# Attention followed by a soft mixture of experts: a new order of all engines, chosen PSUM banks and copy engines, and more second buffers

## The chip, the cores and the metric

The kernel runs on one core of a Trainium2 chip. The metric is the device time of one execution in microseconds (us), lower is better. One profiled execution gives the trace; the times beside it are from runs of the same program.

## The reference, cut to what matters

```python
def _attn_ref(q, k, v):                    # 8 batches, 8 heads, 576 positions, 64 channels, fp32
    scores = (1.0 / np.sqrt(D)) * np.matmul(q, k.transpose(0, 1, 3, 2))
    mask = block_i >= block_j              # blocks of 64 positions: 9 block rows, block-causal
    scores = np.where(mask, scores, -1000000000.0)
    ...
    attn = np.exp(scores - max); attn = attn / (attn.sum(-1) + 1e-09)
    return np.matmul(attn, v)

def _moe_ref(x, phi, w1, w2):              # x: 4608 tokens x 512; 8 experts, 4 slots each, F = 1024
    logits = x @ phi                       # 4608 x 32
    d = softmax(logits, axis=0)            # over all tokens
    slot_input = d.T @ x                   # 32 x 512
    for e in range(E):
        slot_out[e] = np.maximum(slot_input[e] @ w1[e], 0.0) @ w2[e]
    c = softmax(logits, axis=1)            # over the slots
    return c @ slot_out
```

The tokens of x are the attention output of all batches, with the heads side by side.

## The kernel before, in words

**Two stages.** The first goes through 32 pairs (8 batches of 4 pairs; a pair is two heads of one batch, side by side in the 128 partitions). The second computes the experts and the output.

**A pair.** TensorE makes the scores in three steps: `qk(m, "7")` (called UA below, line 412) for query blocks 6 and 7, `qkb` (UB, line 433) for blocks 8, 3, 2, 1 and 0, `qk(m, "5")` (UC, line 412) for blocks 4 and 5. VectorE (DVE) takes the row maxima (`rowmax`, line 454), ScalarE (ACT) the exponentials with their sums (`expo`, line 464), GpSimd (POOL) scales the probabilities by the inverse sums (`norm`, line 481). TensorE then transposes the probabilities in four groups, g7, g5, gc and gd (`tr`, line 501), into an even and an odd PSUM bank, and ACT or DVE copies each bank to SBUF (`evac`, lines 339 and 341). From the copies TensorE forms the product with V: `pv` in two halves pv0 and pv1 (line 539), and `pv8` (called pa, line 549) for block 8. `evac_x` copies the results to xT (xa, xb).

**A batch.** After its four pairs come the logits (`part`, `part4`: lines 568 and 579), a running softmax over tokens (`stats`, `stats1`, `stats2`), x with the tokens in the partitions (`xnat`, line 682, and its copies `evac_n`), and the sums over tokens (`slots`, `slots4`: lines 702 and 711). These are spread over the pairs of the next batches; only those of the last batch stand alone at the end of the stage.

**The experts.** 32 pieces of weights, 1 MB each, W0 to W31. W0 to W15 are read by `up` (line 947), W16 to W31 by `down` (line 967). RES pieces have a place of their own in the big SBUF tile `arena` and are loaded during the attention. The rest go where attention's buffers were, in the order of their places, when those are free (lines 818 to 826), and from W24 on where a used piece of `up` was. `emit` (lines 924, 909) forms the output and copies it to a used piece, from where it is written.

**The order** of all engines is written out: every step is put in a list with a number from the table TM (line 66; per pair of a batch, with entries of their own for pairs 0 to 3, as A to D, and for the last two, w and y), the list is sorted, and the engines' queues follow it. Each engine runs its queue in order. EN says which engine makes a copy.

**PSUM** has eight banks of 128x512: two for products (`x`), two for scores (`sc`), a double one for the scores of blocks 8 and 5 (`sc8`), two for transposes (`pt_e`, `pt_o`). In pair 0 the transposes' banks also hold the scores of blocks 3 to 0.

**At the start** eight products of zeros (`warm`, line 380) and later 8 and 12 short ones (`fill`, line 387) have no use in the result. The eight stand at fixed numbers from -50 up:

```python
        for i in range(WARM):
            at(-50 + 0.01 * i, warm, i)
```

Of the kernel before, what the change touches and what calls it, by code (L numbers as in the profile page):

```python
# [8 lines left out]
F32 = mybir.dt.float32  # L9
# [11 lines left out]
NP = H // 2  # L21
# [17 lines left out]
ONE = "82"  # L39
NXT = 6  # L40
WARM = 8
RES = 17
# [3 lines left out]
for name, n in (  # L46
    *((f"x{i}", S) for i in XIN), ("kr", S), ("q0", S), ("ks0", S), ("p7_0_0", 512), ("p7_1_0", 512),
    ("p5_0_0", 384), ("p5_1_0", 384),
    ("p3_0", 256), ("p1_0", 128), ("p0_0", 128), ("q1", S), ("ks1", S), ("p8", 640), ("v0", 640),
    ("p3_1", 256), ("p2", 256), ("p1_1", 128), ("p0_1", 128),  # L50
    *((f"p{t}_{j}_1", 64 * t + 64) for t in (7, 5) for j in range(2)),
    ("v1", 640), ("pt0", PTN), ("pt1", PTN), ("phi", 128),
):
    AREAS[name] = (LATE0, LATE0 + n)
    LATE0 += n
# [31 lines left out]
    16.10454, "UCC": 16.10654, "nm71C": 16.30906, "xbA": 34.86058, "paB": 25.66258, "rm3C": 16.65299, "ogdB":  # L87
# [7 lines left out]
    24.75602, "gcC": 24.75802, "egcC": 24.76002, "ogcC": 24.76202, "gdC": 24.76402, "paC": 24.76602, "ex8D":  # L95
# [946 lines left out]
```

## Time and profile before

| | us |
|---|---|
| three runs | 364.75, 365.13, 367.5 |
| median | 365.13 |
| span of the profiled execution | 363.1 |
| median less that span | 2.0 |

The page gives the profiled execution by its span, from its first to its last instruction; it gives no other time for it. The granted TensorE clock was 0.988 of full speed in the mean. In the rows further down, a matmul of fp32 is four instructions in the trace (x4), a transpose one. "idle before" says what ended an engine's idle time.

### The profile page before, as it was taken

How to read it: one execution, taken by the hardware profiler on the slowest of the kernel's cores; microseconds unless marked ns; L12 is line 12 of the kernel's file. 1: busy time of each engine (PE TensorE's matmuls, PEld its weight loads, DVE VectorE, ACT ScalarE, POOL GpSimd, SP SyncE). 2: the span in 40 equal slices, each digit the busy share in tenths (PEclk: the TensorE clock that was granted, in tenths of full speed). 3: DMA queues.
4: the chain of work that ended last, by engine and by line, in shares of the span. 5: the costliest groups of instructions: out<-in, count | busy, mean ns of one | idle time of the engine just before them, and what ended most of it. 6: DMA issues, size and time to landing. Idle time of an engine off the chain costs nothing.

```text
span 363.1 us, 14318 instructions
## 1 busy us (share of the span) xinstructions
PE 347.6 (96%) x5694; PEld 237.8 (65%) x5694; DVE 269.1 (74%) x756; ACT 268.0 (74%) x855; POOL 205.6 (57%) x473
## 2 busy tenths in 40 slices
PE   8899999999999999999999999999999999999983
PEld 3566676767667767776677676767676766437651
DVE  4877767978897888778877887788778866463442
ACT  3877889887988798879888988898888776022342
POOL 4886577757765776676666666666667473000000
PEclk9999999999999999999999999999999999999995
DMA  6766363754473646553845464626413069999887
GB/s 202 215 190 209 101 190 123 226 172 138 148 281 102 180 134 215 140 177 99 296 136 148 142 226 125 206 72 245 133 47 118 12 237 382 380 422 420 353 340 281
DMA packets 29219, 72.29 MB, mean 199 GB/s; under 512 B 6881, under 2 KB 15201, under 8 KB 24161
## 3 DMA queue, kind: packets, MB, share of 16 engines
q1 hardware_dynamic: 29152, 71.38, 57.1%
q8 instruction: 45, 0.74, 0.8%
q14 instruction: 22, 0.17, 0.1%
HBM read 61.93 MB, written 9.44 MB: 197 GB/s over the span
## 4 chain that ended last, share of the span: by engine, by line
PE 62%; DVE 5%; ACT 1%; issue 1%; POOL 0%; DVEq 0%; ACTq 0%
PE x L539 13%; PE sc L412 10%; PE pt_e L501 9%; PE sc L433 5%; PE x L549 4%; PE so L967 4%; PE hp L947 4%; PE o L924 3%; PE pt_o L501 2%; DVE arena L341 2%; PE x L702 2%; PE x L568 2%; DVE stat L454 1%; PE x L682 1%; PE x L579 1%
## 5 line engine op out<-in xcount | busy, mean ns | idle before, releaser
L481 POOL TENSOR_SCALAR arena<-arena,stat 128x512 f32<-128x512 f32 (+6 forms) x288 | 152.2, 544 | 57.2 <-DVE stat L470 39.0
L464 ACT ACTIVATE arena<-sc,stat 128x512 f32<-128x512 f32 (+6 forms) x282 | 150.5, 546 | 9.0 <-DVE stat L454 7.9
L454 DVE TENSOR_REDUCE stat<-sc 128x1 f32<-128x512 f32 (+4 forms) x251 | 129.8, 543 | 8.5 <-PE sc L433 5.6
L501 PEld LDWEIGHTS pt_e<-ident,arena 64*128 64x128 f32 x789 | 60.9, 138 | 35.9 <-POOL arena L481 13.5
L501 PE MATMUL pt_e<-ident,arena 64*128 64x64 f32 x789 | 75.2, 228 | 5.4 <-DVE arena L341 2.3
L539 PE MATMUL x<-arena 128*64 128x128 f32 (+2 forms) x640 | 76.2, 384 | 0.2
L501 PE MATMUL pt_o<-ident,arena 64*128 64x64 f32 x789 | 74.8, 229 | 0.2
L412 PE MATMUL sc<-arena 64*128 64x512 f32 (+1 forms) x252 | 63.0, 581 | 0.2
L501 PEld LDWEIGHTS pt_o<-ident,arena 64*128 64x128 f32 x789 | 59.7, 138 | 3.2 <-ACT arena L339 2.1
L539 PEld LDWEIGHTS x<-arena 128*64 128x64 f32 x640 | 41.1, 136 | 30.2 <-issue 18.2
L464 ACT ACTIVATION_READ_ACCUMULATOR arena<-sc,stat 128x1 f32 x282 | 58.4, 207 | 0.0
L339 ACT COPY arena<-pt_o 128x384 f32<-128x384 f32 (+1 forms) x87 | 44.4, 510 | 16.6 <-PE pt_o L501 14.4
L341 DVE COPY arena<-pt_e 128x384 f32<-128x384 f32 (+2 forms) x72 | 40.9, 567 | 10.3 <-PE x L539 7.4
L433 PE MATMUL sc<-arena 64*64 64x192 f32 (+2 forms) x752 | 43.3, 341 | 0.2 <-ACT arena L464 0.2
L433 PEld LDWEIGHTS sc<-arena 64*64 64x64 f32 x752 | 36.2, 132 | 8.3 <-ACT arena L464 3.2
L339 ACT COPY arena<-pt_e 128x384 f32<-128x384 f32 (+2 forms) x54 | 26.7, 494 | 16.6 <-PE pt_o L501 14.0
L474 POOL TENSOR_SCALAR stat<-stat 128x2 f32<-128x2 f32 (+1 forms) x96 | 18.7, 195 | 31.3 <-ACT arena L464 26.3
L470 DVE RECIPROCAL stat<-stat 128x2 f32<-128x2 f32 (+1 forms) x96 | 15.4, 167 | 24.5 <-POOL stat L474 23.6
L549 PE MATMUL x<-arena 128*64 128x64 f32 x640 | 25.7, 227 | 0.0
L549 PEld LDWEIGHTS x<-arena 128*64 128x64 f32 x640 | 21.3, 137 | 5.6 <-ACT xn L339 3.3
L373 POOL TENSOR_SCALAR arena<-arena 128x576 f32<-128x576 f32 x32 | 21.5, 671 | 5.9 <-DMA arena<-in_k 3.0
L341 DVE COPY arena<-pt_o 128x384 f32<-128x384 f32 (+2 forms) x39 | 20.6, 528 | 3.9 <-PE pt_o L501 1.7
(167 smaller groups left out, 362.5 us busy)
## 6 DMA issues: line engine op xcount, KB each, us to landing
arena<-in_w SPq DMA_DIRECT2D x32, 1024.0 KB, 6.9
arena<-in_k SPq DMA_DIRECT2D x32, 288.0 KB, 3.3
arena<-in_q SPq DMA_DIRECT2D x32, 288.0 KB, 3.1
arena<-in_v SPq DMA_DIRECT2D x32, 256.0 KB, 3.2
out<-arena SPq DMA_DIRECT2D x7, 1024.0 KB, 5.1
arena<-in_v SPq DMA_DIRECT2D x32, 32.0 KB, 3.2
out<-arena SPq DMA_DIRECT2D x2, 512.0 KB, 4.5
out<-arena SPq DMA_DIRECT2D x4, 256.0 KB, 3.8
```

The costliest lines, as they stand in the source:

```text
L339: nc.scalar.copy(out=out, in_=in_)
L341: nc.vector.tensor_copy(out=out, in_=in_)
L373: nc.gpsimd.tensor_scalar(out=area(f"ks{m % NQB}"), in0=area("kr" if m > 1 else f"ks{m}"), scalar1=SCALE, scalar2=0.0, op0=ALU.mult, op1=A ...
L412: nc.tensor.matmul(scores(t + str(j), m), lhsT=q[r, lo:lo + 128], rhs=k[r, 0:NC[t]], start=True, stop=True)
L433: nc.tensor.matmul(o, lhsT=a, rhs=b, start=True, stop=True)
L454: nc.vector.tensor_reduce(out=st[:, 0, u:u + n], in_=sc, axis=AX.XY if x == "8" else AX.X, op=ALU.max, negate=True)
L464: nc.scalar.activation(out=pr, in_=sc, func=AF.Exp, bias=st[:, 0, u:u + 1], accum_out=st[:, 1, u:u + 1],)
L474: nc.gpsimd.tensor_scalar(out=st[:, 2, c], in0=st[:, 1, c], scalar1=EPS, scalar2=1.0, op0=ALU.add, op1=ALU.mult)
L481: nc.gpsimd.tensor_scalar(out=pr, in0=pr, scalar1=st[:, 2, u:u + 1], scalar2=0.0, op0=ALU.mult, op1=ALU.add)
L501: nc.tensor.transpose(out=trbank(m, g)[i][:, 64 * n:64 * n + 64], in_=prob(m, x)[r, 128 * c:128 * c + 128], identity=ident[r, r],)
L539: nc.tensor.matmul(xps[m, 0][64 * j:64 * j + 64, lo:hi], lhsT=vs(m)[:, j, c, :], rhs=rhs, start=a, stop=z, skip_group_check=True,)
L549: nc.tensor.matmul(xps[m, 1][64 * j:64 * j + 64, 0:64], lhsT=vs(m)[:, j, c, :], rhs=arena[:, lo:lo + 64], start=(c == 0), stop=(c == NQ - 1),)
```

## The change

The tables TM and EN are new: all engines have another order, and many copies another engine. A table BK names the PSUM bank of each kind of step for each kind of pair. The scores of blocks 8 and 2 get a second buffer (`p8_0`, `p8_1`, `p2_0`, `p2_1`), and so do the transposed probabilities (`pt0_0` to `pt1_1`). These take 4096 columns of `arena`; RES goes from 17 to 15, and nine pieces instead of seven are loaded into attention's buffers at the end. WARM and `fill`'s counts are as before.

```diff
-ONE = "82"
+ONE = ""
+NPT = 2
 NXT = 6
 WARM = 8
-RES = 17
+RES = 15
...
-    ("p3_0", 256), ("p1_0", 128), ("p0_0", 128), ("q1", S), ("ks1", S), ("p8", 640), ("v0", 640),
-    ("p3_1", 256), ("p2", 256), ("p1_1", 128), ("p0_1", 128),
+    ("p3_0", 256), ("p1_0", 128), ("p0_0", 128), ("q1", S), ("ks1", S), ("p8_0", 640), ("p8_1", 640), ("v0", 640),
+    ("p3_1", 256), ("p2_0", 256), ("p2_1", 256), ("p1_1", 128), ("p0_1", 128),
...
-    ("v1", 640), ("pt0", PTN), ("pt1", PTN), ("phi", 128),
+    ("v1", 640), *((f"pt{j}_{i}", PTN) for i in range(NPT) for j in range(2)), ("phi", 128),
...
-    "T": 9.2, "lkA": -5.94771, "lqA": -2.81305, "lkB": -10.95031, "lqB": -8.91013, "ksA": 2.22677, "UAA":
...
-        xbk = [ps.tile([128, 512], F32, name=f"x{i}") for i in range(2)]
...
-        scm = [ps.tile([128, 512], F32, name=f"sc{j}") for j in range(2)]
-        scn = ps.tile([128, 1024], F32, name="sc8")
...
-        ptb = [ps.tile([128, 512], F32, name=f"pt_{x}") for x in "eo"]
...
+        duo = [
+            ps.tile([128, 1024], F32, name=f"duo{i}") if i in WIDE else [ps.tile([128, 512], F32, name=f"one{i}{j}") for j in range(2)]
+            for i in range(4)
+        ]
...
+        def bank(key, z):
+            return BK.get(key + z, BK.get(key))
...
         def warm(i):
             if i == 0:
-                xps["w"] = xbank("pb")
+                xps["w"] = one(0)
...
         def trbank(m, g):
-            return scm if m == NB * NP - 1 and g in ("gc", "g5") else ptb
+            return two(bank("T" + g, sfx(m)))
...
         def evac(m, g, i):
-            lo = AREAS["pt0"][0]
+            lo = AREAS[f"pt0_{m % NPT}"][0]
...
-                pt = arena[:, AREAS[f"pt{j}"][0]:AREAS[f"pt{j}"][1]]
+                pt = area(f"pt{j}_{m % NPT}")
```

Of the new table, `WIDE = (2,)`; in pairs 4 to 29 (kinds .0 to .3) the scores stand in banks 1 (`one10`, `one11`) and 2 (`duo2`), the transposes in 3 (`one30`, `one31`), the products in `one00` (for pa of one kind in `one01`), which are the places that `sc`, `sc8`, `pt` and `x` were.

**TensorE, from the start.** `idle` are the zeros of `warm` and `fill`; sc and sc8 (now one1 and duo2) hold scores, x0 (now one00) the product's bank. Before:

```order
L380 LDWEIGHTS idle_78
L380 MATMUL x0_106<-idle_78 128x512
...
L412 MATMUL sc0_108<-arena_58 128x512
L412 MATMUL sc1_109<-arena_58 128x512
L433 MATMUL sc8_110<-arena_58 64x288 x2
...
L412 MATMUL x0_106<-arena_58 128x384
L412 MATMUL x1_107<-arena_58 128x384
L387 LDWEIGHTS idle_78
L387 MATMUL x0_106<-idle_78 128x128
```

Now:

```order
L448 MATMUL one10_108<-arena_58 128x512
L448 MATMUL one11_109<-arena_58 128x512
L469 MATMUL duo2_110<-arena_58 64x288 x2
...
L415 LDWEIGHTS idle_78
L415 MATMUL one00_106<-idle_78 128x512
...
L448 MATMUL one00_106<-arena_58 128x384
L448 MATMUL one01_107<-arena_58 128x384
L422 LDWEIGHTS idle_78
L422 MATMUL one00_106<-idle_78 128x128
```

UA and UB of pair 0 stand ahead of the warm-ups now. Six warm-ups follow, then UA of pair 1, UC of pair 0, both runs of `fill`, the last two warm-ups and UB of pair 1.

**VectorE, in pairs 0 and 1.** The first two rows are maxima of pair 0's blocks 5, the rows stat1 those of pair 1's UB; a copy of 2x4x64 empties a bank of pair 0's g7. Before:

```order
L454 TENSOR_REDUCE stat0_113<-x0_106 128x1
L454 TENSOR_REDUCE stat0_113<-x1_107 128x1
L341 COPY arena_58<-pt_e_111 128x2x4x64
L454 TENSOR_REDUCE stat1_114<-sc8_110 128x1
L454 TENSOR_REDUCE stat1_114<-sc0_108 128x1
L454 TENSOR_REDUCE stat1_114<-sc1_109 128x1
L341 COPY arena_58<-pt_e_111 128x320
```

Now:

```order
L491 TENSOR_REDUCE stat0_113<-one00_106 128x1
L491 TENSOR_REDUCE stat0_113<-one01_107 128x1
L491 TENSOR_REDUCE stat1_114<-duo2_110 128x1
L491 TENSOR_REDUCE stat1_114<-one10_108 128x1 x2
L491 TENSOR_REDUCE stat1_114<-one11_109 128x1 x2
L507 RECIPROCAL stat0_113<-stat0_113 128x2
L507 RECIPROCAL stat1_114<-stat1_114 128x2
L376 COPY arena_58<-one30_111 128x2x4x64
L376 COPY arena_58<-one31_112 128x2x4x64
```

Both copies of g7 are VectorE's now (the odd one was ScalarE's), and both stand behind all maxima of pair 1's UB.

**VectorE, after the last batch's logits.** bm are the batch's maxima, xn the tokens' x, fident the merge, dn the dispatch weights. Before:

```order
L596 TENSOR_REDUCE bm_7_5335<-x1_107 128x1
L597 TENSOR_REDUCE bm_7_5335<-x1_107 128x1
L626 STREAM_TRANSPOSE c_all_80<-lt_7_5333 128x128
L627 STREAM_TRANSPOSE c_all_80<-lt_7_5333 64x32
L604 TENSOR_TENSOR mrun1_91<-mrun0_90,bm_7_5335 128x2
L605 TENSOR_TENSOR bm_7_5335<-mrun1_91,mrun0_90 128x2
L341 COPY xn_119<-sc8_110 128x8x64
L651 TENSOR_REDUCE fident_95<-sc0_108 1x32
L654 COPY fident_95<-fident_95 1x96
L341 COPY dn_120<-pt_e_111 128x96
```

Now:

```order
L633 TENSOR_REDUCE bm_7_5337<-one00_106 128x1
L634 TENSOR_REDUCE bm_7_5337<-one00_106 128x1
L763 SCALAR_TENSOR_TENSOR acc4_82<-acc4_82,bm_6_4919,duo2_110 128x128
L641 TENSOR_TENSOR mrun1_91<-mrun0_90,bm_7_5337 128x2
L642 TENSOR_TENSOR bm_7_5337<-mrun1_91,mrun0_90 128x2
L376 COPY xn_119<-one10_108 128x8x64
L376 COPY xn_119<-one30_111 128x4x64
L376 COPY xn_119<-one31_112 128x4x64
L689 TENSOR_REDUCE fident_95<-one10_108 1x32
L692 COPY fident_95<-fident_95 1x96
L376 COPY dn_120<-one00_106 128x96
```

The two transposes of the logits have gone behind the end of this chain; a sum of the batch before and two copies of xn have come into it.

## Rows read from the trace of the kernel before

**Rows 1.** The page, part 1: busy us (share of the span), instructions.

```profile
PE 347.6 (96%) x5694; PEld 237.8 (65%) x5694; DVE 269.1 (74%) x756; ACT 268.0 (74%) x855; POOL 205.6 (57%) x473
```

**Rows 2.** Windows: stretch, its length, busy us by engine, PE clock, DMA share, GB/s.

```profile
147.00:183.75 36.75, 36.25 (x613) 25.94 (x611) 30.36 (x87) 31.19 (x103) 25.01 (x57) 1.00 0.57 184
294.00:311.30 17.30, 16.24 (x264) 11.03 (x260) 11.88 (x34) 9.09 (x27) 7.45 (x17) 1.00 0.94 372
311.30:350.40 39.10, 38.59 (x712) 21.47 (x712) 16.78 (x32) 11.24 (x22) 0.00 (x0) 1.00 0.93 382
350.40:354.00 3.60, 2.36 (x19) 1.37 (x19) 1.41 (x5) 1.37 (x5) 0.00 (x0) 1.00 0.94 383
354.00:363.10 9.10, 3.37 (x24) 1.79 (x24) 2.43 (x6) 1.91 (x5) 0.00 (x0) 0.51 0.71 283
```

**Rows 3.** Timeline, TensorE's start: start, us, engine, line, operation, out<-in, count, idle before.

```profile
0.99 3.60 PE L380 MATMUL x<-idle 128*128 128x512 bf16 x8 [0.99 <-DVE mrun L252]
4.51 1.88 PE L412 MATMUL sc<-arena 64*128 64x512 f32 x4
6.32 0.46 PE L433 MATMUL sc<-arena 64*64 64x288 f32 x2
7.57 0.92 PE L412 MATMUL x<-arena 64*128 64x384 f32 x4
8.42 0.62 PE L387 MATMUL x<-idle 128*128 128x128 bf16 x8
8.97 1.13 PE L412 MATMUL sc<-arena 64*128 64x512 f32 x4
10.03 0.84 PE L387 MATMUL x<-idle 128*128 128x128 bf16 x12
12.62 1.31 PE L433 MATMUL sc<-arena 64*64 64x256 f32 x20 [0.24 <-ACT arena L464]
15.69 0.80 PE L549 MATMUL x<-arena 128*64 128x64 f32 x20
17.69 1.11 PE L412 MATMUL sc<-arena 64*128 64x512 f32 x4
```

**Rows 4.** The chain that ended last, UB in the middle: start, us, what.

```profile
131.71 1.25 PE sc L433 x16
```

**Rows 5.** Timeline, DVE in pairs 0 and 1.

```profile
12.87 0.68 DVE L341 COPY arena<-pt_e 128x512 f32<-128x512 f32 x1
13.54 1.09 DVE L454 TENSOR_REDUCE stat<-sc 128x1 f32<-128x576 f32 x3
15.07 0.41 DVE L454 TENSOR_REDUCE stat<-sc 128x1 f32<-128x256 f32 x1
16.34 0.35 DVE L454 TENSOR_REDUCE stat<-sc 128x1 f32<-128x192 f32 x1
```

**Rows 6.** Timeline, TensorE: gd waiting in pairs 0, 1, 5 and 14.

```profile
15.17 0.24 PE L501 MATMUL pt_e<-ident,arena 64*128 64x64 f32 x1 [0.78 <-DVE stat L470]
24.04 0.27 PE L501 MATMUL pt_e<-ident,arena 64*128 64x64 f32 x1 [0.51 <-ACT arena L339]
60.44 0.24 PE L501 MATMUL pt_e<-ident,arena 64*128 64x64 f32 x1 [0.60 <-ACT arena L339]
143.62 0.24 PE L501 MATMUL pt_e<-ident,arena 64*128 64x64 f32 x1 [0.34 <-DVE arena L341]
```

**Rows 7.** The chain that ended last, after the last batch's logits.

```profile
304.95 0.33 ACT lt L339
305.31 0.29 DVE bm L596
305.73 0.22 DVE c_all L626
305.96 0.22 DVE c_all L627
```

**Rows 8.** Timeline, SP's DMA issues at the end.

```profile
293.48 26.03 SPq L284 DMA_DIRECT2D arena<-in_w  x15
```

More of the change, by code (lines that the diff above doesn't have):

```diff
@@ L290, in tile_attention_softmoe, with one, two, sfx @@
         ps = c1.enter_context(tc.tile_pool(name="ps", bufs=1, space=PSUM))
-        xbk = [ps.tile([128, 512], F32, name=f"x{i}") for i in range(2)]
-        scm = [ps.tile([128, 512], F32, name=f"sc{j}") for j in range(2)]
-        scn = ps.tile([128, 1024], F32, name="sc8")
-        ptb = [ps.tile([128, 512], F32, name=f"pt_{x}") for x in "eo"]
-        def xbank(key, z=""):
-            return xbk[EN["X" + key + z]]
+        duo = [
+            ps.tile([128, 1024], F32, name=f"duo{i}") if i in WIDE else [ps.tile([128, 512], F32, name=f"one{i}{j}") for j in range(2)]
+            for i in range(4)
+        ]
+        def one(i):
+            d, j = duo[i // 2], i % 2
+            return d[:, 512 * j:512 * j + 512] if i // 2 in WIDE else d[j]
+        def two(i):
+            return [one(2 * i), one(2 * i + 1)]
+        def sfx(m):
+            return late(m) or f".{m % NP}"
+        def bank(key, z):
+            return BK.get(key + z, BK.get(key))
+        scm = two(1)
+        for t, i in sorted({(k[1], i) for k, i in BK.items() if k[:2] in ("S5", "S7")}):
+            for x in two(i) if EN["Q" + t] == "q" else ():
+                nc.vector.memset(x[0:64, NC[t] - 64:NC[t]], NEG)
         def endz(b):
-            return "z" * (b == NB - 1)
+            return {NB - 1: "z", NB - 2: "v"}.get(b, "")
         def area(name):
@@ L320, in pads @@
                 return
-            for x, n in (("8", 640), ("2", 256), ("0_0", 128), ("0_1", 128)):
+            for x, n in (("8_0", 640), ("2_0", 256), ("8_1", 640), ("2_1", 256), ("0_0", 128), ("0_1", 128)):
                 nc.gpsimd.memset(area("p" + x)[:, NC[x[0]]:n], 0.0)
@@ L393, in scores @@
         def scores(x, m):
-            if m == 0 and x[0] == "5":
-                return xbk[int(x[1])][:, 0:384]
+            z = sfx(m)
             if x == "8":
-                return scn.rearrange("p (n c) -> p n c", n=2)[:, :, 0:288]
-            if x[0] == "5":
-                j = int(x[1])
-                return scn[:, 512 * j:512 * j + 384]
-            if x[0] == "7":
-                return scm[int(x[1])]
+                return duo[bank("S8", z)].rearrange("p (n c) -> p n c", n=2)[:, :, 0:288]
+            if x[0] in "57":
+                return two(bank("S" + x[0], z))[int(x[1])][:, 0:NC[x[0]]]
             j, lo = {"3": (0, 0), "0": (0, 256), "2": (1, 0), "1": (1, 192)}[x]
-            return (scm if m else ptb)[j][:, lo:lo + NC[x]]
+            return two(bank("SB", z))[j][:, lo:lo + NC[x]]
         def qk(m, t):
             q, k = area(f"q{m % NQB}"), area(f"ks{m % NQB}")
-            for j in range(2):
-                r = slice(64 * j, 64 * j + 64)
-                lo = {"7": 0, "5": 128}[t]
-                nc.tensor.matmul(
-                    scores(t + str(j), m), lhsT=q[r, lo:lo + 128], rhs=k[r, 0:NC[t]], start=True, stop=True
-                )
+            lo, n = {"7": 0, "5": 128}[t], NC[t]
+            if EN["Q" + t] == "h":
+                todo = [(slice(0, 128), 0, n)]
+            else:
+                todo = [(slice(0, 64), 0, n - 64), (slice(64, 128), 0, n)]
+            for o, a, e in todo:
+                for j in range(2):
+                    r = slice(64 * j, 64 * j + 64)
+                    nc.tensor.matmul(
+                        scores(t + str(j), m)[o, a:e], lhsT=q[r, lo + o.start:lo + o.stop], rhs=k[r, a:e], start=True, stop=True
+                    )
         def qkb(m):
@@ L424, in qkb @@
                 for i in range(2):
-                    halves[i].append((scn[r, 512 * i:512 * i + 288], q[r, 512:576], k[r, 288 * i:288 * i + 288]))
+                    halves[i].append((scores("8", m)[r, i, :], q[r, 512:576], k[r, 288 * i:288 * i + 288]))
                     o = slice(64 - 64 * j, 128 - 64 * j)
@@ L440, in rowmax @@
             st, u = stat[m % 2], COL[x if x != "5" else "50"]
-            if x == "5":
-                if m:
-                    todo = [(u, 2, scn.rearrange("p (j c) -> p j c", j=2)[:, :, 0:384])]
-                else:
-                    todo = [(u + j, 1, scores(f"5{j}", m)) for j in range(2)]
-                for _, n, sc in todo:
-                    nc.vector.memset(sc[0:64, :, 320:384] if n == 2 else sc[0:64, 320:384], NEG)
+            if x == "5" and bank("S5", sfx(m)) in WIDE:
+                todo = [(u, 2, duo[bank("S5", sfx(m))].rearrange("p (j c) -> p j c", j=2)[:, :, 0:384])]
+            elif x == "5":
+                todo = [(u + j, 1, scores(f"5{j}", m)) for j in range(2)]
             else:
                 todo = [(u, 1, scores(x, m))]
-                if x[0] == "7" and tm(m, "rm" + x) == min(tm(m, "rm70"), tm(m, "rm71")):
+            if EN.get("Q" + x[0]) == "h":
+                if x == "5":
+                    for _, n, sc in todo:
+                        nc.vector.memset(sc[0:64, :, 320:384] if n == 2 else sc[0:64, 320:384], NEG)
+                elif (tm(m, "rm" + x), x) == min((tm(m, f"rm7{j}"), f"7{j}") for j in range(2)):
                     for j in range(2):
-                        nc.vector.memset(scm[j][0:64, 448:512], NEG)
+                        nc.vector.memset(scores(f"7{j}", m)[0:64, 448:512], NEG)
             for u, n, sc in todo:
@@ L522, in pv @@
         def pv(m, i):
-            first = tm(m, f"pv{i}") < tm(m, f"pv{1 - i}")
+            first = (tm(m, f"pv{i}"), i) < (tm(m, f"pv{1 - i}"), 1 - i)
             if first:
-                xps[m, 0] = xbank("pb")
+                xps[m, 0] = one(bank("PB", sfx(m)))
             for j in range(2):
-                pt = arena[:, AREAS[f"pt{j}"][0]:AREAS[f"pt{j}"][1]]
+                pt = area(f"pt{j}_{m % NPT}")
                 if i == 0:
@@ L544, in pv8 @@
         def pv8(m):
-            xps[m, 1] = xbank("pa", "y" * (m == NB * NP - 1))
+            xps[m, 1] = one(bank("PA", sfx(m)))
             for c in range(NQ):
                 for j in range(2):
-                    lo = AREAS[f"pt{j}"][0] + PT8 + 64 * c
+                    lo = AREAS[f"pt{j}_{m % NPT}"][0] + PT8 + 64 * c
                     nc.tensor.matmul(
@@ L562, in part @@
         def part(b, p):
-            z = "z" * (b == NB - 1)
+            z = endz(b)
             order = sorted(range(NP), key=lambda i: TM[f"prt{i}{z}"])
             if p == order[0]:
-                mo[b, "xlg"] = xbank("lg", endz(b))
+                mo[b, "xlg"] = one(bank("LG", endz(b)))
             for g in range(4):
@@ L631, in natural @@
                 r = slice(64 * i, 64 * i + 64)
-                nc.tensor.transpose(out=ptb[i][:, o:o + 64], in_=dt[r, lo:lo + 128], identity=ident[r, r])
+                nc.tensor.transpose(out=two(bank("ND", endz(b)))[i][:, o:o + 64], in_=dt[r, lo:lo + 128], identity=ident[r, r])
         def dispatch(b):
+            ptb = two(bank("ND", endz(b)))
             copy("dn", dn[:, 0:3, :], ptb[0][:, 0:96].rearrange("p (i s) -> p i s", s=NS), endz(b))
@@ L673, in xnat @@
         def xnat(b, i):
-            bk = xbk if b < NB - 1 else (scm, (scn[:, 0:512], scn[:, 512:1024]), ptb)[i]
+            bk = two(bank(f"N{i}", endz(b)))
             mo[b, "xxn", i] = bk
@@ L696, in slots @@
         def slots(b):
-            p0 = xbank("si", endz(b)) if b != NB - 2 else scn[:, 0:512]
+            p0 = one(bank("SI", endz(b)))
             mo[b, "xsi"] = p0
@@ L707, in slots4 @@
         def slots4(b):
-            p0 = xbank("si4") if b != NB - 2 else ptb[0][:, 256:384]
+            p0 = one(bank("S4", endz(b)))
             mo[b, "xsi4"] = p0
@@ L789, in tile_attention_softmoe @@
             if k[-1] == "z":
-                at(tb + TM[k] + 0.0005, fill, scm[1], n)
+                at(tb + TM[k] + 0.0005, fill, one(FZ), n)
             else:
@@ L793, in tile_attention_softmoe @@
         for (m, k), n in FILL0.items():
-            at(m * T + tm(m, k) + 0.00002, fill, xbk[0][:, 384:512], n)
+            at(m * T + tm(m, k) + 0.00002, fill, one(FB)[:, 384:512], n)
         for i in range(RES):
```

36 lines of the change are left out of this document (20 added, 16 removed), and 242 rows, old and new, of tables (BK, EN, TM).

## The prediction

> **What bounds the kernel now.** I read the page's busy times first. TensorE is busy 96% of the span, DVE and ACT 74% each, POOL 57% [rows 1]: see that one engine is near full and two others have a quarter to spare. A mean hides stages, so I read windows next. One round of four pairs in the middle takes 36.75 us, and TensorE is busy 36.25 us of it at the full clock [rows 2]. So in the middle TensorE can give back at most 0.5 us a round, whatever the other engines do; the order can only remove its idle time, since the products and transposes are the same ones. From 294 to 311.3 us TensorE is busy 16.2 of 17.3 us, and in the experts 38.6 of 39.1 [rows 2]. Only the last 12.7 us are loose (2.4 of 3.6 us, then 3.4 of 9.1 at a granted clock of 0.51) [rows 2], and the change leaves that code as it is. What is left is the start, before TensorE is full, and the hand-over to the experts. I read these in the timelines of TensorE and DVE and in the chain of waits.
>
> **The change, part by part.**
>
> *The warm-ups at the start.* Before, eight products of zeros run while the first q and k are on their way, from 0.99 to 4.51 us, where UA of pair 0 starts [rows 3]. They cost nothing there. UA still takes 1.81 us (4.51 to 6.32), against 1.06 for the next one (8.97 to 10.03) and 1.11 for the third, so it runs at the lower level of 1.2 GHz; UB takes 1.25 us (6.32 to 7.57) [rows 3], as in the middle of the kernel [rows 4], so by then the clock is at 2.4 GHz. Now UA and UB come first. Nothing that they wait for is earlier, so UA starts at 4.51 us again, with no work done before it. UB then costs 1.25 us at the upper level or 2.50 at the lower one; these are the bounds. I take 2.50, since the nearest row, UA, ran at the lower level even after eight products. The Trainium skill, TensorE: Matmul & The Clock Gate, section What's actually happening, says that the default state is the throttled one and that activity releases it; by that rule UB costs the 2.50 as well, and by the lower bound of the rows the start would be 1.25 us cheaper.
>
> The warm-ups now have to run while work waits behind them. The eight took 3.5 us at the lower level, 0.44 each; six cost 2.6 us there or 1.3 at the upper. I take 1.3. Then come UA of pair 1 (1.06), UC of pair 0 (0.85, 7.57 to 8.42), both fills (0.55 and about 0.8 us) [rows 3] and two warm-ups (0.4). UB of pair 1 can start at 4.5 + 1.8 + 2.5 + 1.3 + 1.06 + 0.85 + 1.35 + 0.4 = 13.8 us. Before, it got going at 12.62 us, held by ACT [rows 3]: **1.2 us later** (bounds 0, where ACT holds it anyway, and 2.6).
>
> *Copies behind the maxima.* g7 of pair 0 fills both transpose banks, and gd cannot write there until both are empty. Before, ACT emptied one and DVE the other, at 12.87 us, ahead of the maxima of pair 1's UB [rows 5], and gd got through at 15.17 us [rows 6]. Now both copies are DVE's and stand behind all five maxima. UB of pair 1 ends at 13.8 + 1.25 = 15.05. The maxima take 1.09 for three, 0.41 and 0.35 [rows 5], two small reciprocals some 0.3, the copies 0.68 each [rows 5]: gd is free at 15.05 + 1.85 + 0.3 + 1.36 = 18.6 us. Between gd's going on at 15.17 and UA of pair 2 at 17.69 lie 2.5 us before, with pa (0.80) and UC (0.85) in them [rows 3], so 0.9 for gd and g5. Now UA of pair 2 comes at 18.6 + 0.9 = 19.5, 1.8 us later than 17.69, and with pa (0.8) still to do. **The start is 2.6 us behind** (this contains the 1.2). TensorE is nearly full from there on, so the lag is kept unless a later wait of before goes. Bounds: 0, where these copies find DVE free earlier, and 4, where UB is at the late end of its bounds.
>
> *Pairs 1 to 5.* In pairs 1, 2 and 5 gd follows gc directly into the same banks and waits for gc's copies: 0.51 us in pair 1, 0.60 in pair 5 [rows 6]. The new order puts UC, UB or half of pv between them, or takes other banks. In pairs 1 to 3 the new order also puts copies of gc and g5 behind maxima on DVE, the same pattern as above, so I count gain against loss there: 0 (from -1.0, both waits gone, to +1.0, a wait of the size of one copy and one maximum more). In pair 5: **-0.6 us**.
>
> *The middle.* TensorE's order is nearly the same, with pv's halves or `part`s exchanged, and gc ahead of UB in one pair of four; in every kind of pair the banks are those of before, under new names. ACT and DVE have 24 copies each per round, before and now. The second buffers of p8, p2 and pt remove waits that POOL, ACT and DVE may have, but no wait of TensorE that the windows show. The one clear wait there, 0.34 us before gd in the fourth pair of a round [rows 6], keeps its order and its banks. So 0; bounds -0.34 and +0.34 for each of six rounds, -2.0 and +2.0, since nothing excludes a new wait of that size.
>
> *The last batch.* After the last logits the chain goes through DVE. It waits 0.36 us for ACT's copy of the logits, and two transposes take 0.45 [rows 7]. Both leave the chain now: -0.8. A sum of 0.25 and two copies of 256 columns (about 0.4 each by the copy of 512, 0.68 [rows 5]) come into it: +1.05. I take **+0.2** (bounds -0.8 and +1.05).
>
> *Two more late pieces of weights.* They are 2 x 1.05 MB, at 372 to 382 GB/s about 5.5 us of transfers in a stretch that moves data at a share of 0.94 and 0.93 of all DMA engines [rows 2]. SP issued the 15 pieces from 293.48 us over 26 us [rows 8], as places came free. What is idle there is 6% of 17.3 and 7% of 39.1 us, 3.8 us in all. The new order hands the first four places over early (x, k, q and the first pt buffer), so I let the cover hold: 0. Without it, 5.5 - 3.8 = 1.7 us remain, and these would push the output's writes at the end.
>
> Sum: 2.6 + 0 - 0.6 + 0 + 0.2 + 0 = **+2.2 us** on the profiled execution's span of 363.1 us. The median, 365.13 us, is 2.0 above that span; I add the 2.2 to it: 367.3 us. A change of less than 1% (3.65 us) is about what a measurement of this kernel cannot tell from none.
>
> **The rivals.**
>
> *The splits pay and the copies are in time.* The lag of the start stops at UB's 1.2 us, because DVE finishes its maxima earlier than my row-by-row walk, and TensorE has other transposes to do. Then the waits of pairs 1, 2 and 5 go (-1.6, pair 2 counted like pair 1) and half of the middle's (-1.0): 365.13 - 1.4 = 363.7 us, not slower. It decides where UA of pair 2 starts before about 18.5 us. For it: DVE has a quarter of its time free [rows 1]. Against it: DVE runs in order, and those two copies cannot pass the maxima. If the middle's 0.5 us a round go entirely as well, 361.3.
>
> *The clock.* The start now has TensorE waiting more often: for DVE's copies before gd, for ACT before UC. At the end of the kernel the granted clock fell to 0.51 after a stretch in which TensorE was busy 2.4 of 3.6 us [rows 2]. If the same happens around 16 to 20 us, or if the upper level is not reached until then, some 4 to 5 us of products take twice as long: 367.3 + 4 = 371.3 us. The Trainium skill, TensorE: Matmul & The Clock Gate, section HAM oscillation, warns of just this: gaps between groups of matmuls close the gate, and the next group starts cold. By that rule this rival's time holds; in the trace of before the start has waits too (0.78 us before gd in pair 0 [rows 6]), and its later products show the upper level, which speaks against.
>
> *DMA sets the end.* The last pieces come 1.7 to 5.5 us later and the output's writes behind them; the share of 0.71 after 354 us [rows 2] takes 2.6 us of that up. 367.3 + 1.7 to 2.9, say 369.4 us. Against it: the experts read their pieces in the order of loading, and 15 of 17 places are free when they were before.
>
> **How the numbers follow.** My forecast, the lag kept: 0.50, 367.3 us, its own range 365.8 to 369.0. Splits pay: 0.24, 361.3 to 365.0. Clock: 0.13, 370 to 372. DMA: 0.10, 368.8 to 370.2. Something that no row shows: 0.03. The range that leaves out a tenth on each side is 364.2 to 370.6 us. Slower than 368.8: the clock, most of DMA and a tenth of the forecast, 0.28. Faster than 361.5: a quarter of the splits' case, 0.07. Within 1%: 0.65.
>
> **What would show it.** UB of pair 0 in the new timeline at 2.5 or 1.25 us; UB of pair 1 at 13.8; the wait before gd of pair 0, on DVE's copies; UA of pair 2 at 19.5. A round in the middle at 36.75 us. The last weight piece and the writes behind it no later than before, measured from the start of the experts. I am wrong if the start is not behind by two us when pair 4 begins, or if rounds in the middle change by more than 0.3 us: then some wait that I took for fixed work of TensorE was not.

## The result, and the profile after

The changed kernel takes **368.16 us** (median of 4 runs, 367.55 to 371.41), the kernel before 365.15 beside it: the ratio is 1.0101, with a 95% interval of 1.0069 to 1.0134. The forecast was 367.3, with a range of 364.2 to 370.6. The profiled execution after took 368.23 us, with a span of 366.5 (366.45 in the trace, 363.13 before, so 3.3 longer).

The page of the changed kernel, part 1, answers to [rows 1]:

```profile
PE 345.8 (94%) x5694; PEld 239.3 (65%) x5694; DVE 271.6 (74%) x768; ACT 263.8 (72%) x843; POOL 205.8 (56%) x475
```

TensorE does the same 5694 instructions in 1.8 us less of busy time, while the span grows, so its share falls. The windows after, each over the stage that [rows 2] shows for before (length, busy us of PE, PEld, DVE, ACT, POOL, clock, DMA share, GB/s):

```profile
147.00:183.75 36.75, 36.07 (x611) 26.10 (x611) 30.06 (x87) 30.59 (x100) 24.82 (x57) 1.00 0.50 158
297.10:314.20 17.10, 15.36 (x274) 10.49 (x270) 11.35 (x36) 8.10 (x23) 6.70 (x13) 1.00 0.98 402
314.20:353.30 39.10, 38.51 (x704) 21.43 (x705) 17.59 (x34) 11.20 (x22) 0.29 (x1) 1.00 1.01 414
357.00:366.50 9.50, 2.73 (x32) 1.50 (x28) 2.80 (x6) 2.37 (x6) 0.00 (x0) 0.81 0.74 298
```

The middle and the hand-over have more idle time on TensorE, and in the experts the DMA share is now full (0.93 before). TensorE's start in the timeline after, which answers to [rows 3]:

```profile
5.13 2.08 PE L448 MATMUL one<-arena 64*128 64x512 f32 x4 [5.13 <-POOL arena L357]
7.14 0.74 PE L469 MATMUL duo<-arena 64*64 64x288 f32 x2
9.48 2.34 PE L415 MATMUL one<-idle 128*128 128x512 bf16 x6
11.75 1.77 PE L448 MATMUL one<-arena 64*128 64x512 f32 x8
15.11 0.70 PE L469 MATMUL duo<-arena 64*64 64x288 f32 x3
19.40 0.96 PE L538 MATMUL one<-ident,arena 64*128 64x64 f32 x23 [0.26 <-DVE arena L376]
20.14 1.21 PE L448 MATMUL one<-arena 64*128 64x512 f32 x4
21.77 0.80 PE L586 MATMUL one<-arena 128*64 128x64 f32 x20
```

The last two rows are UA of pair 2 and pa of pair 0, which before stood ahead of that UA [rows 3]. Read the differences of successive starts: UA 2.0 us, UB 2.34 (7.14 to 9.48), the six warm-ups 2.27. The record of the granted clock begins at full speed at 11.29 us (6.06 before). The copies of g7 on DVE, which answer to the first of [rows 5]:

```profile
18.07 1.27 DVE L376 COPY arena<-one 128x512 f32<-128x512 f32 x2
```

gd waits for their end. In the middle, two of the waits, before gc in the second pair of a round and before gd in the third:

```profile
170.66 0.53 PE L538 MATMUL one<-ident,arena 64*128 64x64 f32 x10 [0.15 <-DVE arena L376]
182.90 0.49 PE L538 MATMUL one<-ident,arena 64*128 64x64 f32 x9 [0.51 <-DVE arena L376]
```

The first is new and shows in every second round; the second is that of [rows 6] at 143.62 us, and it is longer (0.33 to 0.44 in the five rounds from pair 8 to 28 before, 0.50 to 0.51 after). All of TensorE's idle time from pair 8 to 28 is 2.4 us before and 3.1 after. In the last batch DVE and POOL after show this:

```profile
307.38 0.34 DVE L763 SCALAR_TENSOR_TENSOR acc<-acc,bm,duo 128x128 f32<-128x128 f32 x1
307.63 0.88 DVE L641 TENSOR_TENSOR mrun<-mrun,bm 128x2 f32<-128x2 f32 x1
308.62 1.35 DVE L376 COPY xn<-one 128x512 f32<-128x512 f32 x3
```

```profile
307.33 1.16 POOL L296 TENSOR_TENSOR c_all<-c_all,mx 128x576 f32<-128x576 f32 x1 [2.16 <-DVE mx L295]
```

SP after, the late pieces, which answers to [rows 8]:

```profile
296.27 26.23 SPq L308 DMA_DIRECT2D arena<-in_w  x17
```

The late pieces start 2.8 us later than before. Measured from siT (the last copy ahead of the experts), the last piece lands after 28.9 us, 26.4 before.

The marks below are starts in the timelines of TensorE (siT: its copy on DVE; last write: its landing). The first column is us before, the others are what each kernel is later (+) or earlier (-) there. E1 and so on are the experiments that follow. Each column is one execution: those of E1 and E3 were 0.9 and 1.0 us longer than their medians, that of E10 0.8 shorter.

| mark | before | after | E1 | E2 | E3 | E5 | E6 | E10 |
|---|---|---|---|---|---|---|---|---|
| UA, pair 2 | 17.69 | +2.45 | +0.17 | +3.44 | +0.10 | -0.31 | -0.27 | -0.87 |
| UA, pair 5 | 44.79 | +1.52 | -0.63 | +3.46 | +0.13 | -1.29 | -1.20 | -1.84 |
| UA, pair 8 | 72.31 | +1.43 | -0.73 | +3.47 | +0.20 | +0.72 | +0.47 | -1.93 |
| UA, pair 28 | 256.47 | +3.10 | +1.03 | +3.48 | +0.18 | +0.62 | +0.39 | -0.27 |
| part4, last batch | 304.26 | +1.91 | -0.15 | +3.50 | +0.11 | +1.48 | +1.51 | -1.45 |
| siT | 311.03 | +2.80 | +0.74 | +3.49 | +0.10 | +1.47 | +1.50 | -1.04 |
| last write | 362.17 | +3.32 | +2.37 | +3.81 | +1.85 | +2.23 | +2.19 | -0.36 |

At UA of pair 2 the new start (all columns but before, E2 and E3) still has pa of pair 0 to do, 0.74 us by the starts in [rows 3]; from pair 5 on all have the same products and transposes behind them. UA of pair 5 after is the second of these rows, and the first is UC of pair 4. Two expectations below took their figures for pair 5 (45.59 us, and a gain of 2 us) from UC:

```profile
45.59 0.89 PE L448 MATMUL duo<-arena 64*128 64x384 f32 x4
46.32 1.02 PE L448 MATMUL one<-arena 64*128 64x512 f32 x4
```

So the loss has four places: 1.4 us by pair 8, 1.7 over the five rounds to pair 28 (a third of a us each), 0.9 between part4 and siT, and 0.5 behind siT; between pair 28 and part4 1.2 come back. The last of the four is within the spread of single executions: E1 has the same code behind siT and loses 1.6 there.

### The profile page after: what moved, and what is told of

It is laid out like the page before. It is cut to its first block, busy times and chain, and to the rows that moved or that the text cites. A ratio compares the mean times of both kernels' runs of the same rounds, so it can differ in the third digit from the quotient of the medians.

```text
span 366.5 us, 14434 instructions
## 1 busy us (share of the span) xinstructions
PE 345.8 (94%) x5694; PEld 239.3 (65%) x5694; DVE 271.6 (74%) x768; ACT 263.8 (72%) x843; POOL 205.8 (56%) x475
## 4 chain that ended last, share of the span: by engine, by line
PE 68%; DVE 14%; ACT 8%; POOL 4%; issue 3%; DMA 1%; DVEq 0%; ACTq 0%; POOLq 0%
PE one L576 13%; PE one L538 13%; PE one L448 6%; DVE stat L491 6%; ACT arena L501 6%; PE one L469 5%; PE so L1005 4%; PE duo L448 4%; PE one L586 4%; PE hp L985 4%; PE duo L469 4%; DVE arena L376 3%; PE o L962 3%; POOL arena L518 2%; PE one L605 2%
## 5 line engine op out<-in xcount | busy, mean ns | idle before, releaser
L501 ACT ACTIVATE arena<-one,stat 128x512 f32<-128x512 f32 (+5 forms) x194 | 94.0, 498 | 10.9 <-DVE stat L491 10.2
L374 ACT COPY arena<-one 128x384 f32<-128x384 f32 (+2 forms) x138 | 66.4, 504 | 26.3 <-PE one L538 25.7
L538 PEld LDWEIGHTS one<-ident,arena 64*128 64x128 f32 x1588 | 65.0, 138 | 30.6 <-issue 11.5
L376 DVE COPY arena<-one 128x384 f32<-128x384 f32 (+3 forms) x135 | 72.0, 547 | 15.1 <-PE one L538 14.0
L538 PE MATMUL one<-ident,arena 64*128 64x64 f32 x1588 | 75.4, 228 | 4.3 <-DVE arena L376 3.8
L491 DVE TENSOR_REDUCE stat<-one 128x1 f32<-128x512 f32 (+5 forms) x194 | 76.8, 439 | 3.4 <-PE one L469 1.7
L576 PE MATMUL one<-arena 128*64 128x256 f32 (+2 forms) x640 | 76.3, 384 | 0.0
L501 ACT ACTIVATE arena<-duo,stat 128x384 f32<-128x384 f32 (+1 forms) x94 | 59.3, 635 | 17.9 <-DVE stat L507 10.5
L491 DVE TENSOR_REDUCE stat<-duo 128x1 f32<-128x576 f32 (+1 forms) x63 | 53.8, 855 | 20.3 <-PE duo L469 18.5
L576 PEld LDWEIGHTS one<-arena 128*64 128x64 f32 x640 | 40.9, 137 | 31.9 <-issue 18.3
L586 PEld LDWEIGHTS one<-arena 128*64 128x64 f32 x620 | 20.6, 137 | 9.5 <-ACT arena L374 4.2
```

The costliest lines, as they stand in the source:

```text
L374: nc.scalar.copy(out=out, in_=in_)
L376: nc.vector.tensor_copy(out=out, in_=in_)
L491: nc.vector.tensor_reduce(out=st[:, 0, u:u + n], in_=sc, axis=AX.XY if x == "8" else AX.X, op=ALU.max, negate=True)
L501: nc.scalar.activation(out=pr, in_=sc, func=AF.Exp, bias=st[:, 0, u:u + 1], accum_out=st[:, 1, u:u + 1],)
L538: nc.tensor.transpose(out=trbank(m, g)[i][:, 64 * n:64 * n + 64], in_=prob(m, x)[r, 128 * c:128 * c + 128], identity=ident[r, r],)
L576: nc.tensor.matmul(xps[m, 0][64 * j:64 * j + 64, lo:hi], lhsT=vs(m)[:, j, c, :], rhs=rhs, start=a, stop=z, skip_group_check=True,)
```

## The experiments

Each ran in five rounds beside the kernel before, whose medians there were 365.0 to 365.4 us.

**E1: warm-ups first again.**

```diff
-            at(-50 + 0.01 * i, warm, i)
+            at(-300 + 0.01 * i, warm, i)
```

> The changed kernel with one number undone: all eight warm-ups stand ahead of UA of pair 0 again. Theory A (the late warm-ups cost what the start shows and the lag is carried on): UB of pair 0 takes 1.25 us instead of 2.34, UA of pair 1 starts at about 9 us instead of 11.75, and of these 2.7 us some 2 are still there when pair 8 begins (UA of pair 8 at 71 instead of 73 us): 366.0 us. Rival B (pairs 1 to 5 of the new order have slack, and DVE's maxima and copies set their pace, not the start of TensorE): UA of pair 1 is as early, but UA of pair 5 comes at most 0.8 us earlier than in the changed kernel (45.59 us): 367.4 us or more.

Measured: 366.45 us, ratio 1.0024 (1.0002 to 1.0047). Theory A holds: UA of pair 8 comes 2.2 us earlier than after, and the time falls by 1.7. TensorE's timeline (gd of pair 0, UA of pair 2) bears on what the copies behind the maxima cost:

```profile
17.11 0.96 PE L538 MATMUL one<-ident,arena 64*128 64x64 f32 x23 [0.26 <-DVE arena L376]
17.86 1.16 PE L448 MATMUL one<-arena 64*128 64x512 f32 x4
```

gd still waits 0.26 us for DVE, and yet UA of pair 2 is 0.17 us from its old place. With pa counted the start is 0.9 us behind here and 3.2 in the changed kernel, so most of its loss was the warm-ups. In the other six runs with the warm-ups first and this start the mark lies between -0.97 (E8) and -0.27 (E6), so the copies cost little. From pair 2 to 5 the new order then gains 1.5 us, pa counted.

**E2: late warm-ups alone, in the kernel before.**

```diff
-            at(-50 + 0.01 * i, warm, i)
+            at(5.43 + 0.0001 * i, warm, i)
```

> The kernel before with one number changed: the eight warm-ups stand behind UB of pair 0 instead of ahead of UA. Theory A (the lag of a late start is carried to the end, TensorE being full from there): UA of pair 0 at 4.5, UB in about 2.4 us, the eight warm-ups in 2 to 3.5 us, UC and UA of pair 1 some 3 us later than before, and UA of pair 8 still 2 us later: 367.2 us. Rival B (the old order's pairs 0 to 4 wait for DVE and ACT anyway and take the lag up): UA of pair 5 within 0.5 us of before: 365.4 us.

Measured: 368.39 us, ratio 1.0078 (1.0059 to 1.0098). UA of pair 1 is 3.45 us late, and from there to siT the lag lies between 3.44 and 3.50 us at every mark: the old order has no slack to take it up, and rival B falls. Theory A was right, with its time 1.2 us too small.

**E3: buffers alone, in the kernel before.**

```diff
-ONE = "82"
+ONE = ""
+NPT = 2
-RES = 17
+RES = 15
```

(and the tiles' second names and places as in the change)

> The kernel before with the second buffers for the transposed probabilities and for the blocks 8 and 2, and with 15 resident and 9 late pieces, in the old order throughout. Theory A (buffers alone change nothing ahead of the experts, and the two further late pieces cost a part of their 5.5 us at the end): UA of every pair within 0.3 us of before, the last weight piece lands about 5 us later (342.5 instead of 337.4), and the end is 0.5 to 1.0 us later: 365.9 us. Rival B (the pieces are hidden altogether, as forecast): 365.2 us. Rival C (no cover at all): 366.9 us. Rival D (the buffers take waits off ACT, DVE and POOL that TensorE feels): below 364.8 us.

Measured: 365.73 us, ratio 1.0015 (1.0000 to 1.0029). The middle does not move, so rival D falls. The last piece lands at 339.83 us instead of 337.40, and the time rises by 0.3 us (by the interval at most 1.1): between A and B.

**E4: the old middle in the new kernel.**

```diff
+TM.update({k: v - 3.5 for k, v in OLD.items()})
+EN.update(OLD_EN)
+BK.update({"PA.1": 0, "SI": 1})
```

(OLD holds the rows of the table before for the four kinds of pairs and for batches 0 to 5, OLD_EN their copy engines.)

> The changed kernel with the order, copy engines and banks of the middle (pairs 4 to 29 and batches 0 to 5) taken from the kernel before; start, hand-over and buffers stay. Theory A (the new order of the middle costs the 0.3 us a round that the two traces differ by): UA of pair 28 minus UA of pair 8 takes what it took before, 183.3 us instead of 185.0, and the whole is 1.7 to 1.9 us shorter: 366.4 us. Rival B (the drift comes from the second buffers, which lie at other places of the arena, or from something that the order does not set): the middle stays at 185.0 us and the whole at 368.2.

Measured: 379.33 us, ratio 1.0379 (1.0354 to 1.0403). Its time says nothing: the seams cost 3.8 us between pairs 4 and 6 and 7.0 at pair 30, and a late v 1.6 at pair 19. Between these it answers the question. From pair 8 to pair 19 it takes 101.71 us, against 101.63 before and 102.55 after. The lengths in the expectation are too low by 0.85 us (from pair 8 to 28 it is 184.17 before and 185.83 after), and the rounds named below by 0.2; the differences on which they rest are as given. The second seam shows something else. TensorE's two waits there, and windows around them (length, PE busy, clock, DMA share, GB/s):

```profile
283.72 0.58 PE L842 MATMUL one<-ident,arena 64*128 64x64 f32 x12 [1.84 <-DVE arena L680]
284.96 0.34 PE L842 MATMUL one<-ident,arena 64*128 64x64 f32 x1 [0.66 <-ACT arena L678]
```

```profile
278.00:284.36 6.36, 4.46 (x96) 1.00 0.49 144
284.36:291.19 6.83, 4.87 (x46) 0.50 0.00 0
291.19:298.00 6.81, 6.78 (x101) 1.00 0.15 46
```

After a stretch in which TensorE was busy 4.46 of 6.36 us, with the wait of 1.84 us in it, the clock fell to one half, for 6.83 us in the midst of the kernel.

**E5: new start, old order from pair 6 on; E6: the seam at pair 5.**

```diff
-FIRST = {0: "A", 1: "B", 2: "C", 3: "D"}
...
+TM.update({k: v - 3.8 for k, v in OLD.items()})
...
+TM.update({k: v - 3.8 for k, v in END.items()})
...
+FIRST = {0: "A", 1: "B", 2: "C", 3: "D", 4: "E", 5: "F"}
...
-            at((4 + 3.2 * i) / 2 * T, load_piece, i, arena[:, o:o + PIECE])
+            at((4 + 3.2 * i) / 2 * T - 3.8 * (i > 2), load_piece, i, arena[:, o:o + PIECE])
```

(E and F are the new rows for pairs 4 and 5, and E6 has E alone and four steps at its seam 0.6 to 0.8 us earlier; END holds the old rows for the last two pairs and batches; engines and banks go with them. Warm-ups first, second buffers kept. In E5 the last pair's sums and the slots of batch 6 share a bank, which changes that part of the computation.)

> The second buffers, the warm-ups first, the new order, banks and copy engines for pairs 0 to 5, and the old ones from pair 6 to the end (hand-over included). Theory A (the new order gains some 0.8 us by pair 6 and the old one neither gains nor loses behind it): UA of pair 6 at 53.4 us, UA of pair 28 at 255.7 (0.8 ahead of before), the experts start 0.8 us earlier than before, and the end is that of the buffers alone less 0.8: 364.9 us. Rival B (the drift is not the order's but comes with the second buffers being used): the middle loses 0.3 us a round here too, 366.4 us. Rival C (the seam between the two orders costs as much as the new start gains): UA of pair 8 level with before, 365.7 us.

> As the kernel with the new start and the old rest, with the seam at pair 5, the copy engines and keys at it chosen so that no transposes wait for the copy of the logits (1.23 us at 52.78 us there), and the sixth-last sums of the sums for slots in a bank of their own. Theory A (the new order of the first pairs gains 2 us by pair 5, and only the seam gave it back): UA of pair 8 at 71.3 us, 1.0 ahead of before; UA of pair 28 still 1.0 ahead; 364.8 us. Rival B (the gain of the first pairs is borrowed: work of DVE and ACT that the new order puts off has to be done by pair 8 in whatever order follows): UA of pair 8 level with before (72.0 to 72.6), 365.7 us, which is the time of the buffers alone.

Measured: 367.13 us, ratio 1.0060 (1.0039 to 1.0080), and 367.05 us, 1.0056 (1.0035 to 1.0076). In both the middle is flat: 184.06 and 184.08 us from pair 8 to 28. With E3 this settles the drift: neither the buffers nor the start make it, so what is left is the order of the middle with its copies (and two of its banks, see E10). In E5 one wait at the seam is plain,

```profile
54.01 0.34 PE L1246 MATMUL one<-ident,xT 64*128 64x64 f32 x3 [1.23 <-DVE lt L902]
```

but E6, without it, is 0.47 us behind at pair 8 all the same, about as its rival B said: the old order does not keep the 1.2 to 1.3 us that the new start has gained by pair 5. Both lose another 0.9 to 1.1 us between pair 28 and part4, which I did not follow, so their times lie above all that was expected.

**E7: the softmax over c_all earlier.**

```diff
+TM.update({"comb0z": 332.1 - 257.6, "comb1z": 350.15 - 257.6})
```

> The changed kernel with one edit: the two parts of the softmax over the first half of c_all stand ahead of the last batch's copies on DVE instead of between them and the maxima of the logits. Theory A (DVE's minimum into mrun takes 0.88 us because POOL multiplies c_all at that time; 0.16 us in the kernel before, where POOL was idle): the minimum takes 0.2 us, siT is copied 0.6 to 1.2 us earlier, 367.4 us. Rival B (the minimum waits for the maxima or for ACT's copy of the logits): it takes 0.9 us still and the end stays at 368.2. Rival C (the moved parts now delay POOL's scaling or DVE's copies for the last pair): part4 starts later than 306.2 us and the end is 368.2 or more.

Measured: 367.55 us, ratio 1.0061 (1.0039 to 1.0083). DVE and POOL in this kernel:

```profile
306.33 0.34 DVE L764 SCALAR_TENSOR_TENSOR acc<-acc,bm,duo 128x128 f32<-128x128 f32 x1
306.58 0.15 DVE L642 TENSOR_TENSOR mrun<-mrun,bm 128x2 f32<-128x2 f32 x1
```

```profile
303.71 1.16 POOL L297 TENSOR_TENSOR c_all<-c_all,mx 128x576 f32<-128x576 f32 x1 [2.46 <-DVE mx L296]
```

With POOL idle beside it the minimum takes 0.15 us, much as before, where POOL's operation had ended at 305.34 us:

```profile
306.20 0.16 DVE L604 TENSOR_TENSOR mrun<-mrun,bm 128x2 f32<-128x2 f32 x1
```

From part4 to siT it is now 6.83 us, against 7.66 after and 6.77 before: theory A, and nearly the whole loss of the hand-over. In the changed kernel POOL's operation ended at 308.49 us and the minimum at 308.51. The Trainium skill, SBUF — State Buffer, section SBUF: two separate sides, says that a DVE operation with two inputs in SBUF and one of GpSimd that reads SBUF shut each other out for the whole instruction; the trace agrees. The sum into acc, one of whose two tensors is in PSUM, took 0.34 us beside POOL and 0.34 without it.

**E8: three fixes; E9: a copy ahead in addition.**

```diff
+TM["gc.1"] = 18.74
+TM.update({"comb0z": 332.1 - 257.6, "comb1z": 350.15 - 257.6})
+TM.update({"mg1z": 384.5 - 257.6, "stats2z": 380.0 - 257.6})
```

(on E1; E9 has `TM["eg5.2"] = TM["rm5.3"] + 9.2 - 0.001` as well)

> The changed kernel with three edits, one in each stage, so that each can be read from its own stretch: the warm-ups ahead of UA of pair 0 (as in the first experiment), gc of the second pair of each round back behind UB (key of gc.1), and in the last batch both parts of the softmax over the first half of c_all moved ahead of the last xT copies, with mg1 ahead of the last xn copy on DVE and the exponentials ahead of a copy on ACT. Theory A (each wait named in the comparison is the cause of its loss): a round takes 36.80 us instead of 36.95, since gc no longer waits 0.14 us for DVE's copy; the minimum into mrun takes 0.2 us instead of 0.88, and from part4's start to siT's copy 6.6 us instead of 7.7; together with the start 364.8 us. Rival B (waits move: gd takes the wait of gc, and another operation on DVE the 0.7 us): round and hand-over as in the first experiment, 366.4 us. Rival C (the stream of late pieces and writes sets the end whatever comes before): the hand-over gains its 1 us and the end does not, 365.7 us.

> The kernel with three fixes and one more edit in the middle: in one pair of four DVE copies g5's transposes (eg5.2) ahead of the maxima of block 5 of the next pair, not behind them. Theory A (g7 comes 0.14 us late behind UA in that pair because its banks wait for this copy): UA of the first pair of a round to g7 takes 0.99 us instead of 1.13, a round 36.65 to 36.70 us. Rival B (the maxima then come 0.5 us later, and the exponentials and transposes behind them): a round 36.9 us or more, 0.7 us or more lost over the middle.

Measured: 371.55 us, ratio 1.0178 (1.0156 to 1.0201), and 375.14 us, 1.0275 (1.0252 to 1.0298). Both theories A fell. From pair 8 to 28 E8 takes 190.03 us and E9 192.89, against 185.92 in E1. With gc behind UB a round is 0.8 us longer, and a wait stands before the next transposes in its place, on ACT; with the copy ahead of the maxima 0.6 more, and a wait for another copy. Here they are, one from each kernel:

```profile
96.24 0.47 PE L541 MATMUL one<-ident,arena 64*128 64x64 f32 x8 [0.46 <-ACT arena L377]
```

```profile
112.42 0.65 PE L580 MATMUL one<-arena 128*64 128x256 f32 x4 [0.58 <-DVE xT L380]
```

Taking away the wait that one sees did not take away the loss: in this order gc belongs ahead of UB. The reordered hand-over took 7.56 us from part4 to siT, against 6.83 with the softmax moved alone.

**E10: the new order mended.**

```diff
-            at(-50 + 0.01 * i, warm, i)
+            at(-300 + 0.01 * i, warm, i)
...
+TM.update({"comb0z": 332.1 - 257.6, "comb1z": 350.15 - 257.6})
+BK.update({"PA.1": 0, "SI": 1})
```

> The changed kernel with the warm-ups first, the softmax over the first half of c_all earlier, and two banks of the middle as before (pa of the second pair of a round in bank 0 of PSUM, the slots in bank 1). Theory A (the two banks have to do with the drift of 0.3 us a round): rounds of 36.75 us or less, 365.0 us. Rival B (the drift is that of the order and of the copies' places in DVE's and ACT's queues; the banks don't matter): rounds of 36.95 us as in the changed kernel, the two other edits add up: 368.2 - 1.7 - 0.6 = 365.9 us.

Measured: 365.31 us, ratio 1.0009 (0.9996 to 1.0023). From pair 8 to 28 it takes 185.83 us, so the two banks do not matter (rival B). The gains of the other two edits add up to 365.8 us (1.7 and 0.6 off 368.2); the run came out 0.5 below that. With them the changed kernel can no longer be told from the kernel before.

**E11: the first late piece earlier in E10; E12: the same in the kernel before.**

```diff
-    *((f"x{i}", S) for i in XIN), ("kr", S), ("q0", S), ("ks0", S), ("p7_0_0", 512), ("p7_1_0", 512),
+    ("q0", S), ("ks0", S), ("p7_0_0", 512), ("p7_1_0", 512), ("p3_0", 256), ("p1_0", 128), ("p0_0", 128), ("p2_0", 256),
...
```

> The mended new order (warm-ups first, softmax earlier, two banks) with the tiles of the arena laid out in another order, so that the place of the first late piece is free once q, k and block 7 of pair 30 have been read, not only after the last reading of x of batch 6. Theory A (with nine late pieces the stream of pieces and output writes, back to back from the first late piece to the last write, sets the end): the first late piece is issued at about 289.2 us instead of 292.9, directly behind the last load of v, pieces and writes land 1 to 2.5 us earlier, and the time is 364.1 us, below the kernel before. Rival B (the experts' products and the last writes, which are issued as results come, set the end): the pieces land earlier and the end stays: 365.3 us.

> The kernel before with the same new layout of the arena and nothing else. Theory A (with seven late pieces the stream runs dry before the experts release the next place, 24 pieces and all, so an earlier first piece only makes the gap longer): the first late piece is issued at about 290 us instead of 293.5, the eighth one still at 312.5 when the experts begin, and the time stays at 365.1 us. Rival B (the start of the stream sets the end here too): 363.5 to 364.3 us.

Measured: 364.21 us, ratio 0.9982 (0.9960 to 1.0004), and 365.17 us, 1.0003 (0.9991 to 1.0014): the times of theory A in both. SP's issues of the late pieces in E10, E11 and E12:

```profile
292.91 26.37 SPq L310 DMA_DIRECT2D arena<-in_w  x17
```

```profile
289.33 28.52 SPq L309 DMA_DIRECT2D arena<-in_w  x17
```

```profile
289.61 29.60 SPq L283 DMA_DIRECT2D arena<-in_w  x15
```

The same 3.6 to 3.9 us bring 1.1 us where nine pieces are late (all runs of E11 but one lie below all of E10) and nothing where seven are. The traces show less of it. E11's last piece lands 2.9 us before E10's and its last write 0.9, and 0.4 of this stands already at siT, where TensorE in E10 has a gap of 0.42 us that is not in E11. That the stream of pieces sets the end is thus supported, but not shown. The 364.21 is the lowest median of the study, but its interval takes in 1.

## Why the prediction held, point by point

- **The start, 2.6 behind: measured 3.2.** The 2.6 were 1.8 at UA of pair 2 and 0.8 for pa; the trace has 2.45 and 0.74. E7, which has the same start, has 1.59 there, so the forecast lies inside the spread of single executions. Its make-up was not right. UB of pair 0 at half clock: forecast 2.50, measured 2.34. I gave the six warm-ups 1.3 us at the upper level; they took 2.27, since the clock rose only at 11.29 us, and UA began 0.62 late. UB of pair 1 came at 15.11, not 13.8. To the copies behind the maxima I gave the other 1.4; the runs with the warm-ups first, where they stand in the same place, are 0.9 behind at most, pa counted (E1).
- **The lag is kept: half right.** E2 shows it kept to the end in the old order. In the new one pairs 2 to 4 give back 1.7 us, pa counted (1.52 left at pair 5; E1: 1.5). I had put pairs 1 to 3 at 0, between -1.0 and +1.0: outside the bounds. UA of pair 4 is 1.21 us late (1.95 with pa; 0.36 and 1.10 in E7), so the first of my two signs of being wrong, a start not behind by two us when pair 4 begins, came true, narrowly here and plainly in E7.
- **Pair 5, -0.6: not seen.** From pair 5 to 8 the lag changes by 0.1 us (1.52 to 1.43). UC of pair 6 now has a wait of the same size as gd's [rows 6], 0.60 us, for ACT's exponentials; after, in TensorE's timeline:

```profile
63.05 0.92 PE L448 MATMUL duo<-arena 64*128 64x384 f32 x4 [0.60 <-ACT arena L501]
```

- **The middle, 0 with bounds of 2.0: measured +1.7 from pair 8 to 28.** This is the term that was mis-sized. I had named a change of up to 0.34 us a round as the bound, and it came nearly in full: from 36.83 us (I read 36.75) to 37.17. A change by more than 0.3 us was my second sign of being wrong, so the argument that the middle is fixed work of TensorE does not stand. Its idle time explains 0.7 of the 1.7 us (3.1 against 2.4); the rest lies in its busy time, where I can read no wait. What remains open is which places in DVE's and ACT's queues do it: two single edits made it worse, the two banks that differ from before (I had written that none does) changed nothing (E10), and no other was tried.
- **The last batch, +0.2: measured +0.9 from part4 to siT.** POOL's hold on the minimum, 0.73 us (0.88 against 0.15), is a term that I had left out; without it (E7) the stretch is 0.06 longer than before. Ahead of it the last pairs gave back 1.2 us that no term had.
- **Two late pieces, 0 (1.7 without cover): measured 0.3 alone (E3).** In the new kernel the last piece lands 2.5 us later than before, measured from siT, where I had said no later; the last write is 0.5 later. The mended kernel gains 1.1 with an earlier first piece (E11). So a part of the DMA rival may be true.
- **The clock as a rival** did not come as I put it: the level stayed full from 11.29 to 362.86 us. It rose later than before (6.06), though, and that is in the first point. E4 shows a fall in the midst of a kernel. By the Trainium skill, TensorE: Matmul & The Clock Gate, section HAM oscillation, gaps between groups of matmuls close the gate. E4's trace agrees (0.50 for 6.83 us, after a wait of 1.84 us); at the start of the changed kernel the waits for DVE and ACT were 0.20 and 0.26 us, and the level stayed full.
- **A slip in a rival.** The splits' best case, by its own terms, is 365.13 + 1.2 - 1.6 - 3.0 = 361.7 us, not 361.3.

Against the working, the trace shows 0.6 us less at pair 8, 1.7 more in the middle, 1.2 less by part4, 0.7 more by siT and 0.5 more behind it: 3.3 instead of 2.2. The time was right in part by luck: errors of both signs met, while both of the signs that I had named for being wrong came true.

## What to carry to other kernels

On an engine that is full, a lag at the start can stay to the end (in E2 it kept within 0.06 us), so idle work such as warm-ups belongs ahead of the first real work. The wait that a profile names is where a loss is seen, and need not be where it is made: in E8 moving the waiting step cost five times what its wait was. Two good stretches of different lists lost 1.7 to 7 us where they met (E4, E5, E6).

## What the runs showed of the hardware

- The same first instructions met the clock's rise at different times. In E1, E8 and E9, which share their start, the record of the full level begins at 6.81, 4.00 and 5.38 us, with the first product at 0.99 in each, and UA of pair 5 follows it: 44.16, 42.87 and 43.39. The changed kernel and E7, which also share a start, have the full level from 11.29 and 10.00 us, and UA of pair 2 at 20.14 and 19.28. So a start in one profile is good to about 0.7 us, and E10's -1.84 in the table holds some of this luck (full level from 4.11 us).
- The level at the end varies as well: the last emits ran at half speed from 354.22 us before, and mostly at full speed after (0.81 in the window above).
